# Four changes to the order of a fused linear-attention and maxout kernel: stores with slack, scores and y in pairs, wo's second half last, the last output in halves

## The chip, the cores and the metric

The kernel runs on one core of one Trainium2 chip. The metric is device time in microseconds (us) of one execution. Each kernel is executed several times; a run is called slow when it is more than 1.5% above the fastest of the same kernel, and only fast runs go into a ratio. Faster or slower asks for 2%.

A profile records one execution. Its span is shorter than the measured time by about 1.8 us, and it may fall on a run that is not typical.

## The reference, cut to what matters

```python
def _attn_ref(q, k, v, alpha):            # all (4, 8, 768, 48)
    state = zeros((B, H, D, D))
    for t in range(S):
        state = alpha[:, :, t, :, None] * state + einsum('bhd,bhe->bhde', k[:, :, t], v[:, :, t])
        y[:, :, t] = einsum('bhd,bhde->bhe', q[:, :, t], state)

def _moe_ref(x, w1, w2, w_out):           # x (3072, 384), w1 and w2 (384, 1024), w_out (1024, 384)
    return np.maximum(x @ w1, x @ w2) @ w_out

def reference(...):                       # x is y with heads side by side
    x = attn_out.transpose(0, 2, 1, 3).reshape(B * S, H * D)
    return _moe_ref(x, w1, w2, w_out)
```

The kernel cuts the tokens into 24 chunks of 128. In a chunk the recurrence becomes matmuls: cumulative sums of ln alpha (`cs`), transposes of scaled q and k (`tp`), the scores k·q (`pa`, `pb`), a masked copy of them (`pt`), and y from `pt` with v and from the carried state (`T`). The six chunks of the first batch go two at a time, as "double" chunks whose tiles begin with d (`dcs`, `dtp`, `dpa`, `dy`). The maxout uses max(h1, h2) = relu(x(w1 − w2)) + x w2. So it needs one product `h` of 384 × 1024 per token and a relu `g`; the second term is folded into a matrix `m` = w2·wo that is made once (`mp` in PSUM).

## The kernel before: what the change touches

The code in this section is shortened.

All instructions are put in order ahead of time by a small list scheduler. It keeps estimated times for the five engines; for each it picks, among the operations whose inputs and buffers will be ready, the one with the smallest (time, priority).

```python
def pick(self, e):
    now = self.free[e]
    best = None
    for op in self.todo[e]:
        t = self.start(op)
        if t is None:
            continue
        margin = self.MARGIN if e == "PE" and op.prio < 1000 else 0.0
        late = max(t + margin, now)
        key = (late, op.prio - (0.5 if op.tiled and self.tiled else 0.0))
        if best is None or key < best[0]:
            best = (key, max(t, now), op)
    return best
```

Operations marked `tiled` are the scores and y. Their matmuls use parts of TensorE's array (64 × 128 tiles for the scores, 128 × 32 for y); everything else uses the whole of it.

```python
def p3(n):                     # scores of a chunk, tiled=True
    for r in range(NP):
        for o, ps in ((0, pa), (64, pb)):
            nc.tensor.matmul(ps[:, r, :], lhsT=qk[o:o+D, NP+r, :], rhs=qk[o:o+D, r, :], start=True, stop=True)

def p4(n):                     # y of a chunk, tiled=True
    for b, x, is_t, start, stop in rounds(n % NCH == 0):
        ...                    # lhsT is 32 columns of T16 or of v16
        nc.tensor.matmul(y[o:o+32, b//4, :], lhsT=lhsT, rhs=rhs, start=start, stop=stop)
```

The output of 128 tokens takes eleven matmuls of 384 columns, a copy out of PSUM, and a store issued from SP, the queue that issues the loads too:

```python
def tstep(a, i, half):
    if half == 0:
        op = ops[t0] = psm.tile([128, DM], FP32, tag="m", name="op")
        for s in range(3):
            nc.tensor.matmul(op, lhsT=xT[:, s, t0:t0+C], rhs=m16[:, s, :], start=(s == 0), stop=False)
    op = ops[t0]
    for f in (range(3) if half == 0 else range(3, NF)):
        nc.tensor.matmul(op, lhsT=gts[a][:, f, i*C:(i+1)*C], rhs=wo16[:, f, :], start=False, stop=(f == NF-1))

def oevict(e, t0):
    outs[t0] = mo.tile([128, DM], FP32, tag="outs", name="outs", bufs=NO)     # NO = 4
    copy(e, outs[t0], ops[t0])

def store(t0):
    nc.sync.dma_start(out=out[t0:t0+C, :], in_=outs[t0])
```

The big loads have a fixed order, with each weight in two halves; `m` takes eight steps over the halves of w2 and wo:

```python
for x in "d0 w20 w21 wo0 w10 wo1 w11 d1 d2".split():
    ...
def prep_m(s, i):              # i: half of wo
    ...                        # mp: one PSUM tile for both halves
    for f in range(NFH*i, NFH*i + NFH):
        nc.tensor.matmul(mp, lhsT=w2T[:, f, s*128:(s+1)*128], rhs=wo16[:, f, :], start=(f == 0), stop=(f == NF-1))
```

The single chunks' loads of alpha, k, q and v reuse the space of the float32 weights. So in a profile "w2f<-in_alpha" is a load of alpha.

## Time and profile before

| kernel before | us |
|---|---|
| three executions | 148.53, 151.44, 147.98 |
| execution that was profiled | 151.01 |
| span of that profile | 149.2 |

The prediction below shows this profile's lines and reads them. Two things help to read it. The row "PE" of the 40 slices gives TensorE's busy share in tenths. A timeline line gives start, duration, engine, source line, operation, output and inputs, tile shape, operand shape, and how many alike were grouped. Matmuls overlap, so the distance between starts is what one costs, not its duration.

### The profile page before, as it was taken

What the parts mean: (1) busy time and instruction counts of PE and PEld (TensorE: products, weight loads), DVE (VectorE), ACT (ScalarE), POOL (GpSimd) and SP (SyncE); (2) the same over time, 40 slices, a digit from 0 to 9 for tenths busy, and PEclk for the clock granted to TensorE, in tenths of its full rate; (3) what the DMA queues carried; (4) which work ended last, traced back from release to release, by engine and by line L of the source; (5) the groups of instructions that cost most, each with busy time, mean ns of one, the idle gap of its engine ahead of it and who ended that gap; (6) DMA issues with size and microseconds to landing.
All of it is one profiled execution on the core that took longest, in us unless ns stands there. A gap on an engine that the chain in (4) does not pass through costs nothing.

```text
span 149.2 us, 4865 instructions
## 1 busy us (share of the span) xinstructions
PE 131.3 (88%) x1958; PEld 87.7 (59%) x1958; DVE 85.2 (57%) x161; ACT 100.8 (68%) x223; POOL 82.3 (55%) x184
## 2 busy tenths in 40 slices
PE   0275698799998968999999999999999999999990
PEld 0263555676776655766665666665665666656650
DVE  4745764577676676886476766679269693200000
ACT  4431876867784487778767996797768666935721
POOL 7975600769996269774088857657567963000000
PEclk9999999999999999999999999999999999999998
DMA  5989999999969699979899997989999861103112
GB/s 123 244 266 392 380 356 234 244 264 197 195 157 211 134 199 201 236 150 242 195 206 208 226 237 133 211 208 216 199 201 243 191 145 53 53 6 114 43 61 97
DMA packets 93543, 28.62 MB, mean 192 GB/s; under 512 B 87889, under 2 KB 91985, under 8 KB 93521
## 3 DMA queue, kind: packets, MB, share of 16 engines
q1 hardware_dynamic: 93520, 28.32, 80.0%
q8 instruction: 15, 0.25, 0.7%
q14 instruction: 8, 0.06, 0.1%
HBM read 23.59 MB, written 4.72 MB: 190 GB/s over the span
## 4 chain that ended last, share of the span: by engine, by line
PE 68%; SPq 14%; DMA 11%; ACT 2%; issue 1%; POOL 1%; DVE 0%; ACTq 0%; POOLq 0%; DVEq 0%
PE op L711 20%; PE h L694 19%; PE op L708 7%; SPq L203 7%; DMA dqf<-in_q_dram 6%; PE y L465 6%; PE pa L406 3%; DMA w1f<-in_alpha_dram 3%; SPq L223 3%; DMA w2f<-in_alpha_dram 3%; PE tp L388 3%; PE tp L390 2%; PE cs L330 2%; SPq L233 2%; PE kv L417 2%; SPq L194 2%
## 5 line engine op out<-in xcount | busy, mean ns | idle before, releaser
L711 PE MATMUL op<-wo,g 128*128 128x384 f16 x192 | 37.3, 326 | 0.0
L694 PE MATMUL h<-xT,wd 128*128 128x384 f16 (+1 forms) x216 | 36.6, 309 | 0.0
L701 ACT ACTIVATE g<-h 128x384 f16<-128x384 f32 (+1 forms) x53 | 23.8, 469 | 2.7 <-PE h L694 2.4
L694 PEld LDWEIGHTS <-wd 128*128 128x128 f16 x216 | 19.2, 98 | 9.2
L711 PEld LDWEIGHTS <-g 128*128 128x128 f16 x192 | 17.9, 98 | 11.3
L425 DVE TENSOR_TENSOR pt<-pa,u 128x512 f16<-128x512 f32 x18 | 12.4, 690 | 12.0 <-PE pb L406 6.5
L655 ACT COPY outs<-op 128x384 f32<-128x384 f32 x20 | 9.6, 480 | 13.8 <-PE op L711 13.8
L655 ACT COPY qk<-tp 128x1024 f16<-128x1024 f16 x15 | 15.2, 1016 | 1.7 <-PE tp L390 1.5
L367 POOL TENSOR_TENSOR T<-w,g 48x192 f16<-48x192 f32 x30 | 15.6, 520 | 1.2
L708 PE MATMUL op<-m,xT 128*128 128x384 f16 x72 | 15.6, 325 | 0.0
L425 DVE TENSOR_TENSOR pt<-pb,u 128x512 f16<-128x512 f32 x18 | 12.3, 683 | 0.1
L521 POOL TENSOR_TENSOR dkt<-dkf,den 128x384 f16<-128x384 f32 x6 | 6.3, 1058 | 9.8 <-ACT den L503 9.8
L469 ACT CAST xT<-y 128x384 f16<-128x384 f32 x18 | 8.7, 484 | 4.4 <-PE y L465 4.0
L352 POOL TENSOR_TENSOR kt<-wof,en 128x384 f16<-128x384 f32 x6 | 6.3, 1053 | 8.6 <-ACT en L340 6.3
L436 DVE TENSOR_TENSOR w<-kv,t 48x192 f32<-48x192 f32 x24 | 8.5, 353 | 3.9 <-PE kv L417 3.0
L699 DVE TENSOR_SCALAR g<-h 128x256 f16<-128x256 f32 (+1 forms) x19 | 8.6, 475 | 1.8 <-PE h L694 1.8
L340 ACT ACTIVATE en<-cs 128x384 f32<-128x384 f32 x18 | 9.0, 498 | 0.8 <-PE cs L334 0.8
L465 PE MATMUL y<-pt,v 128*32 128x128 f16 x288 | 9.0, 220 | 0.4 <-ACT outs L655 0.4
L340 ACT ACTIVATE ep<-cs 128x384 f32<-128x384 f32 x18 | 9.0, 502 | 0.0
L352 POOL TENSOR_TENSOR kt<-w1f,en 128x384 f16<-128x384 f32 x6 | 6.0, 1003 | 4.9 <-ACT en L340 2.4
L352 POOL TENSOR_TENSOR kt<-w2f,en 128x384 f16<-128x384 f32 x6 | 6.0, 1001 | 4.2 <-ACT en L340 3.3
L708 PEld LDWEIGHTS <-xT 128*128 128x128 f16 x72 | 6.4, 97 | 3.3
(121 smaller groups left out, 273.1 us busy)
## 6 DMA issues: line engine op xcount, KB each, us to landing
out_dram<-outs SPq DMA_DIRECT2D x24, 192.0 KB, 3.0
w2f<-in_moe_w_dram SPq DMA_DIRECT2D x2, 768.0 KB, 7.8
wof<-in_moe_w_out_dram SPq DMA_DIRECT2D x2, 768.0 KB, 11.2
w1f<-in_moe_w_dram SPq DMA_DIRECT2D x2, 768.0 KB, 12.2
dvf<-in_v_dram SPq DMA_DIRECT2D x3, 384.0 KB, 5.6
wof<-in_alpha_dram SPq DMA_DIRECT2D x6, 192.0 KB, 4.0
wof<-in_k_dram SPq DMA_DIRECT2D x6, 192.0 KB, 4.6
wof<-in_q_dram SPq DMA_DIRECT2D x6, 192.0 KB, 4.8
```

The costliest lines, as they stand in the source:

```text
L203: nc.sync.dma_start(out=dloads[m][i][:, hs], in_=src[0, hs, m * C2 : (m + 1) * C2, :].rearrange("h (p j) d -> p h (j d)", j=2),)
L340: nc.scalar.activation(out=t, in_=csv, func=ACTF.Exp, scale=scale)
L352: nc.gpsimd.tensor_mul(out=kts[n % NB][:, :, 0:D], in0=loads[n][1], in1=st[n]["en"])
L367: nc.gpsimd.tensor_mul(out=st[n]["T16"][ps, :, D * t : D * t + D], in0=st[n - 1]["w"][ps], in1=st[n]["g"][ps].unsqueeze(2).to_broadcast([D ...
L425: nc.vector.tensor_mul(out=s["pt"][:, t], in0=s["pp"][t], in1=ub)
L465: nc.tensor.matmul(y[o : o + 32, b // 4, :], lhsT=lhsT, rhs=rhs, start=start, stop=stop)
L469: nc.scalar.copy(out=xT[:, :, n * C : (n + 1) * C], in_=st[n]["y"])
L655: {"ACT": nc.scalar.copy, "DVE": nc.vector.tensor_copy, "POOL": nc.gpsimd.tensor_copy}[e](out=out, in_=in_)
L694: nc.tensor.matmul(h[:, 0:W], lhsT=wd16[:, s, f * 128 : (f + 1) * 128], rhs=xT[:, s, a : a + W], start=(s == 0), stop=(s == 2))
L701: nc.scalar.activation(out=gts[a][:, f, 0:W], in_=hs[a, f][:, 0:W], func=ACTF.Relu)
L708: nc.tensor.matmul(op, lhsT=xT[:, s, t0 : t0 + C], rhs=m16[:, s, :], start=(s == 0), stop=False)
L711: nc.tensor.matmul(op, lhsT=gts[a][:, f, i * C : (i + 1) * C], rhs=wo16[:, f, :], start=False, stop=(f == NF - 1))
```

## The change

Four intentions: (1) a store isn't issued until 3 us after it could be, so that loads overtake it, with six output buffers instead of four; (2) a ready scores or y group is held for up to 2.5 us until a second one is ready, so that both run in one stretch; (3) wo's second half is loaded after all of w1, and the first half of `m` isn't made until the first double chunk's y; (4) the last 128 tokens' output is made in two halves of 192 columns, so that the last copy and the last store are half as big.

```diff
-    def __init__(self, ..., tiled=False, after=()):
+    def __init__(self, ..., tiled=False, after=(), slack=0.0):
+    HOLD = 2.5
 ...
     def pick(self, e):
-        for op in self.todo[e]:
-            t = self.start(op)
+        ready = [(op, self.start(op)) for op in self.todo[e]]
+        hold = e == "PE" and not self.tiled and sum(op.tiled for op, t in ready if t is not None and t <= now + 0.1) < 2
+        for op, t in ready:
 ...
-            late = max(t + margin, now)
-            key = (late, op.prio - (0.5 if op.tiled and self.tiled else 0.0))
+            late = max(t + margin + op.slack, now)
+            prio = op.prio
+            if op.tiled and self.tiled:
+                prio -= 2.0
+            elif op.tiled and hold and now - t < self.HOLD and now > 45.0:
+                prio += 2000.0
+            key = (late, prio)
 ...
+    def tcols(a, i, c):        # half c of the last output: 3 + 8 matmuls of 192 columns
+    def ocols(e, t0, c):       # its copy
+    def scols(t0, c):          # its store: SP for the first half, ACT for the second
+        eng = nc.scalar if c else nc.sync
+        eng.dma_start(out=out[t0 : t0 + C, cs], in_=outs[t0][:, cs])
 ...
-    NG, NO = 3, 4
+    NG, NO = 3, 6
 ...
-    for x in "d0 w20 w21 wo0 w10 wo1 w11 d1 d2".split():
+    for x in "d0 w20 w21 wo0 w10 w11 wo1 d1 d2".split():
 ...
-                      ..., after=[prev],
+                      ..., after=[prev] if i else [],
+            if i == 0:
+                mfirst.append(prev)
 ...
+        if m == 0:
+            for o in mfirst:
+                o.after.append(g["p4", 0])
 ...
+            if a + i == NCG - 1:
+                for c in range(2):
+                    ... tcols, ocols (ACT), scols ...
+                continue
 ...
-            op("st", a + i, {"SP": 0.55}, ..., prio=-1)
+            op("st", a + i, {"SP": 0.55}, ..., prio=-1, slack=3.0 if a + i < NCG - 4 else 0.0)
```

More of the change, by code (lines that the diff above doesn't have):

```diff
@@ L16, with __init__ @@
 class Op:
-    def __init__(self, sched, name, n, engs, fn, deps=(), lat=0.1, alloc=(), reads=(), prio=0.0, tiled=False, after=()):
+    def __init__(self, sched, name, n, engs, fn, deps=(), lat=0.1, alloc=(), reads=(), prio=0.0, tiled=False, after=(), slack=0.0):
         self.name, self.n, self.engs, self.fn, self.lat = name, n, engs, fn, lat
@@ L22, in __init__ @@
         self.after = [d for d in after if d is not None]
-        self.done = None
+        self.done, self.slack = None, slack
         for b in list(alloc) + list(reads):
@@ L93, in pick @@
             margin = self.MARGIN if e == "PE" and op.prio < 1000 else 0.0
-            late = max(t + margin, now)
-            key = (late, op.prio - (0.5 if op.tiled and self.tiled else 0.0))
+            late = max(t + margin + op.slack, now)
[5 more added lines that the diff above has]
+            key = (late, prio)
             if best is None or key < best[0]:
-                best = (key, max(t, now), op)
+                best = (key, max(t + op.slack, now), op)
         return best
@@ L712, in tstep @@
                              start=False, stop=(f == NF - 1))
+    def tcols(a, i, c):
+        t0 = a + i * C
+        cs = slice(c * DM // 2, (c + 1) * DM // 2)
+        op = ops[t0, c] = psm.tile([128, DM], FP32, tag="m", name="opc")
+        for s in range(3):
+            nc.tensor.matmul(op[:, 0 : DM // 2], lhsT=xT[:, s, t0 : t0 + C], rhs=m16[:, s, cs], start=(s == 0), stop=False)
+        for f in range(NF):
+            nc.tensor.matmul(op[:, 0 : DM // 2], lhsT=gts[a][:, f, i * C : (i + 1) * C], rhs=wo16[:, f, cs],
+                             start=False, stop=(f == NF - 1))
+    def ocols(e, t0, c):
+        if c == 0:
+            outs[t0] = mo.tile([128, DM], FP32, tag="outs", name="outs", bufs=NO)
+        copy(e, outs[t0][:, c * DM // 2 : (c + 1) * DM // 2], ops[t0, c][:, 0 : DM // 2])
+    def scols(t0, c):
+        cs = slice(c * DM // 2, (c + 1) * DM // 2)
+        eng = nc.scalar if c else nc.sync
+        eng.dma_start(out=out[t0 : t0 + C, cs], in_=outs[t0][:, cs])
     outs = {}
@@ L795 @@
         w2t.append(op("w2te", f, {"DVE": 0.6, "ACT": 0.75}, lambda e, f=f: prep_te(e, f), deps=[t], reads=[b], prio=-0.4))
-    mdone = []
+    mdone, mfirst = [], []
     for s in range(3):
@@ L801 @@
             prev = op("m", s, {"PE": 0.66}, lambda e, s=s, i=i: prep_m(s, i), lat=0.17,
-                      deps=w2t[2 * i : 2 * i + 2] + woc[2 * i : 2 * i + 2], after=[prev],
+                      deps=w2t[2 * i : 2 * i + 2] + woc[2 * i : 2 * i + 2], after=[prev] if i else [],
                       alloc=[b] if i == 0 else (), reads=[b] if i else (), prio=0.4 + 0.01 * s)
+            if i == 0:
+                mfirst.append(prev)
         mdone.append(op("mev", s, {"ACT": 0.4, "DVE": 0.45}, lambda e, s=s: copy(e, m16[:, s, :], mps[s]),
@@ L970, in refill @@
             bo, bs = Buf(rm), Buf(ro)
+            if a + i == NCG - 1:
+                for c in range(2):
+                    b = (bo, Buf(rm))[c]
+                    o = op("t", a + i, {"PE": 0.95}, lambda e, a0=a0, i=i, c=c: tcols(a0, i, c), lat=0.17,
+                           deps=mdone + woc + rel, after=pend[-1:], alloc=[b], reads=[bg], prio=1000 + a)
+                    pend.append(o)
+                    ev = op("oev", a + i, {"ACT": 0.28}, lambda e, t=a0 + i * C, c=c: ocols(e, t, c), deps=[o],
+                            alloc=[] if c else [bs], reads=[b, bs] if c else [b], prio=n)
+                    op("st", a + i, {"ACT" if c else "SP": 0.3}, lambda e, t=a0 + i * C, c=c: scols(t, c), lat=1.2, deps=[ev],
+                       reads=[bs], prio=-1)
+                continue
             for half in range(2):
@@ L977, in refill @@
                     alloc=[bs], reads=[bo], prio=n)
-            op("st", a + i, {"SP": 0.55}, lambda e, t=a0 + i * C: store(t), lat=1.2, deps=[ev], reads=[bs], prio=-1)
+            op("st", a + i, {"SP": 0.55}, lambda e, t=a0 + i * C: store(t), lat=1.2, deps=[ev], reads=[bs], prio=-1, slack=3.0 if a + i < NCG - 4 else 0.0)
         return True
```

## The prediction

> **What bounds the kernel now.** I read the page's engine shares and 40 slices first, then the busy time by windows, then TensorE's waits, then its timeline at the changes between kinds of matmul, and last the chain of waits and the DMA landings.
>
> The page: the PE row is full from about slice 17 to the last, DMA is full until slice 32.
>
> ```profile
> PE 131.3 (88%) x1958; PEld 87.7 (59%) x1958; DVE 85.2 (57%) x161; ACT 100.8 (68%) x223; POOL 82.3 (55%) x184
> PE   0275698799998968999999999999999999999990
> DMA  5989999999969699979899997989999861103112
> ```
>
> Windows of 5 us (first figure after the length is PE's busy time): idle sits before 30 us and in 45 to 60, and from 60 to 145 there is none.
>
> ```profile
> 25.00:30.00 5.00, 3.85 (x46) 3.10 (x44) 2.79 (x5) 4.33 (x12) 2.94 (x3) 1.00 1.04 249
> 45.00:50.00 5.00, 4.33 (x125) 3.14 (x124) 3.06 (x7) 3.34 (x8) 3.05 (x7) 1.00 0.94 201
> 50.00:55.00 5.00, 3.77 (x58) 2.78 (x56) 3.67 (x8) 2.43 (x8) 2.22 (x6) 1.00 0.74 147
> 55.00:60.00 5.00, 4.39 (x69) 3.00 (x67) 3.42 (x7) 3.80 (x12) 4.23 (x8) 1.00 0.98 212
> 60.00:65.00 5.00, 5.00 (x81) 3.24 (x78) 3.89 (x8) 4.09 (x8) 3.43 (x8) 1.00 0.95 204
> ```
>
> PE's waits in 45 to 60 us are for ln of alpha, for the cast of v and once for a free PSUM bank; behind the first two stand loads (the groups name the DMA of alpha into w2f's and w1f's space and of v). A busy figure that counts overlapping tails hides part of it: by start times PE lost about 0.83 us at 46.4, 1.0 at 52, 0.5 at 53.2 and 0.77 at 57.2, together 3.1 us.
>
> ```profile
> PE cs L330 <- ACT loga L325: 1.3, 2, 0.7
> PE kv L417 <- POOL v L356: 0.9, 1, 0.9
> PE y L465 <- ACT outs L655: 0.4, 1, 0.4
> ```
>
> So the end is the sum of PE's work after 60 us, of what PE loses before 60, and of the tail. But "busy" from 60 on is not all matmul. The timeline shows what a change of tiling costs:
>
> ```profile
> 61.03 0.98 PE L711 MATMUL op<-wo,g 128*128 128x384 f16 x5
> 61.94 0.23 PE L406 MATMUL pa<-qk 48*128 48x128 f16 x1
> ...
> 62.12 0.22 PE L406 MATMUL pb<-qk 48*128 48x128 f16 x1
> 62.27 0.40 PE L388 MATMUL tp<-ident,qt 128*128 128x128 f16 x4
> ...
> 65.35 0.28 PE L465 MATMUL y<-pt,v 128*32 128x128 f16 x5
> 65.56 0.23 PE L406 MATMUL pa<-qk 48*128 48x128 f16 x1
> ```
>
> Output matmuls start every 0.163 us, so five end at 61.84; the scores start at 61.94: 0.10 lost. From the last score (62.12) to the transpose (62.27) is 0.15 where transposes follow each other at 0.056: 0.095 lost. From the last y (65.35 plus 0.28 less its own 0.22, so 65.41) to the scores (65.56) 0.15 again: y (128x32 tiles) and scores (64x128 tiles) differ too. Each change of tile shape costs some 0.095 us, whatever the two shapes.
>
> The tail, from the chain and the landings: last matmul group 144.46 to 145.77, the copy 145.84 to 146.32, the store issued at 146.34, landed at 148.20, span 149.2.
>
> ```profile
> 144.46 1.31 PE op L711 x8
> 145.77 0.03 ACTq L655
> 145.80 0.04 issue
> 145.84 0.48 ACT outs L655
> ```
>
> **What the Trainium skill says.** "TensorEngine Tiling (Array Packing)", section Key Properties: "Changing tiling mode (not just tile) drains the TensorE". The trace agrees and gives the size, 0.095 us. "TensorE: Matmul & The Clock Gate", part 1: the array's clock halves after about 3.4 us idle and returns after as long a busy stretch. Here transposes step at 0.107 us before 21.8 us and at 0.056 later, and no idle of up to 1.1 us brought the slow step back; that matters below. "DMA: Bandwidth & Descriptors", section Issuing engines are not separate DMA queues: DMAs from SP and ACT share the same 16 engines, and a second issuer saves only issue time; before issues from SP alone, so no run here shows it.
>
> **The change part by part.**
>
> *Scores and y together.* A ready tiled group is held up to 2.5 us (after the scheduler's own 45 us) until two are ready; once in tiled mode the bonus is 2 instead of 0.5. I counted changes of tile shape in the two programs' instruction orders: 87 before, 76 after. Before, 7 of the 18 single chunks' score groups stood next to a y; after, all 18 do (14 y then scores, 4 scores then y). 11 x 0.095 = 1.05 us off PE, nearly all after 60 us where PE has no other slack: it comes off the end. Matmul counts are otherwise the same (72 h of 256 and 144 of 384 columns in both).
>
> *Stores with slack.* A store may not be issued until 3 us after it could, except the last four, so loads go first; outs grows from 4 to 6 buffers for it. Where it matters is 41.9 to 43.9: two stores (41.88 and 43.18) stand before chunk 8's alpha (issued 42.66, landed 46.58) and k. After, alpha, k and q of chunk 8 precede the first store. A 192 KB transfer takes 0.65 to 0.95 us of the queue here, so alpha lands one transfer earlier or a little more, about 45.2 to 45.9, and the 0.83 us wait at 46.4 goes. The bytes don't change and DMA is full until 120 us, so by the ninth chunk's alpha (the 36th DMA in both orders, landed 52.67) nothing is gained. The new PE order now asks for exactly that load before anything else: after the common prefix (which ends at 51.7) it has the cumulative sum of chunk 9, where before had scores, kv and y. PE gets there at about 51.3 and can go on at 52.67 + 0.1 + 0.53 (ln) = 53.3: 2.0 us idle, in place of before's 1.0 + 0.5 at nearly the same place, with 0.5 us of work (scores, kv) not yet done. At the next such point (chunk 10's alpha, 57.24 in before) the new order has more to do first and waits about 0.25 in place of 0.77. Together 45 to 60: 3.1 becomes about 2.25, gain 0.85.
>
> *wo's second half last.* w1's second half now lands about 21.1, wo's about 23.9 (before the reverse: 21.07 wo, 23.93 w1). The second 12 matmuls of w2.wo need it: casts end about 24.8 instead of 21.9. The first 12 now run together, to about 23.1 (four at 0.32, eight at 0.163 from 20.48); then PE idles 1.7 us, too short for the clock, and the other 12 x 0.163 end at 26.75. Before, the stream ended at 25.2 and chunk 2's cumulative sums waited for alpha until 25.78. They slip by 0.95; den, dep and POOL's dkt with them. But PE then waited 0.92 for dqt until 28.54, which was held by q's landing (27.83). Now dep ends at 28.3 in place of 27.3, so dqt starts 0.4 later, and PE's transposes start about 28.95: 0.45 lost net. It pays into the wait at 46.4 which the earlier alpha has removed, so I count it whole: +0.45.
>
> *Last tokens by halves.* 11 matmuls of 384 columns become 22 of 192, 0.081 each if the step scales (256 columns step at 0.109): no cost. Copies of 256 columns take 0.39 and of 384 0.49 us in the relu groups, so 192 take about 0.34: 0.15 off the last copy. The last store is half the bytes: full stores took 1.86 us from issue to landing, of which perhaps 0.2 goes. 0.35 us together, all of it on the end. It is issued from ACT, which has nothing else left.
>
> Sum: -1.05 - 0.85 + 0.45 - 0.35 = -1.8 us. Of 148.5 that makes 146.7. I take 146.6, since the schedule was surely picked to be better than this reading of its first part.
>
> **Rivals.** (1) *The hold creates new waits.* PE runs strictly in order; pulling scores next to y ties a chunk's y to its masks on DVE, and the relus on ACT are now clumped. For it: three PSUM banks feed h, op and y. Against: DVE is at 57%, ACT at 68%, the scheduler still asks for 0.25 us of margin per group, and its previous order has no wait at all from 60 on. If each of the 18 pairs waited 0.1, 1.8 us would be back: 148.5, same. (2) *DMA becomes the bound.* It runs at 0.9 to 1.0 until 120 us; if PE is faster the loads don't come faster. Against: PE has 22 us of pure feed-forward after 124 us, so a backlog is there to fill holes; only the start, where there is none, can starve. If the first part loses what the switches gain: 148. (3) *The load phase gains more.* If chunk 9's alpha also lands an us earlier (41 to 43 DMA was at 0.45), the 2.0 us of idle halve: 145.5. (4) *The reordered weights are worse than I think*, the clock falling back in the 1.7 us gap: h and dcs at half speed for 3.4 us would add about 1.5: 148.
>
> **Range and chances.** Switches and tail, 1.4 us, are sure to 0.3. The first 60 us are sure to about 1.2 either way[...]. The runs of before spread from 147.98 to 151.44. So 145.2 to 148.3 for 8 in 10. 2% is 3 us; the sum would need the optimistic first part too: 0.2. Slower by 2% needs both rival 1 and 4: 0.03. Same: 0.77.
>
> **What would show it.** The timeline: y and scores adjacent, 0.15 between them, 3 changes for each pair. Windows 60 to 145 still 5.00 each; if some are at 4.5, rival 1. PE's waits: the one for w2f's alpha at 46 gone, a wait of 1 to 2 us at chunk 9's cumulative sum near 51 to 53 (if absent, rival 3), a gap of 1.7 near 23 to 24.8 before the second half of mp, transposes of chunk 2 at 28.95. The tail: last copy about 0.34, end of the last matmul to the span's end 3.0 in place of 3.4. I am wrong if PE's stretch from 60 to its end is not 1 us shorter in sum of gaps.

## The result, and the profile after

The changed kernel took 146.69 us (median of four runs, 146.62 to 146.77), and the kernel before, beside it, 148.58 (147.98 to 151.44). The ratio of the fast runs is 0.9886 (95% interval 0.9856 to 0.9916). A ratio here is the mean time of one kernel's fast runs over the mean time of the other's fast runs of the same rounds, so it is not quite the ratio of the medians. The predicted time, 146.6 us, was met within 0.1 us. What follows shows that not all of its terms were.

The page of the changed kernel, its summary line of the engines and two rows of the 40 slices:

```profile
PE 129.7 (90%) x1969; PEld 89.4 (62%) x1969; DVE 86.6 (60%) x163; ACT 99.1 (68%) x222; POOL 83.0 (57%) x184
PE   0376884899999999999999999999999999999991
DMA  4999999999989898999997999999899852010213
```

PE has eleven matmuls more (22 narrow ones in place of 11) and is full from slice 9 on. The dent of before in slices 13 to 16 ("8968") is gone.

The same stretch by windows of 5 us, changed kernel (length, then busy time of PE, PEld, DVE, ACT, POOL with their counts, PE's clock, DMA share, GB/s):

```profile
45.00:50.00 5.00, 5.00 (x132) 3.65 (x130) 2.74 (x7) 3.30 (x8) 3.70 (x9) 1.00 0.93 219
50.00:55.00 5.00, 4.82 (x103) 3.88 (x101) 3.99 (x8) 5.00 (x13) 3.76 (x8) 1.00 1.00 194
```

PE is busy for 9.82 us of these ten, where the profile of before had 8.10. That looks like the gain from the earlier loads which the prediction expected. The first experiment shows that it isn't.

The timeline of PE at a pair, changed kernel:

```profile
57.42 0.22 PE L414 MATMUL pb<-qk 48*128 48x128 f16 x1
...
57.53 0.22 PE L414 MATMUL pb<-qk 48*128 48x128 f16 x1
57.68 0.24 PE L473 MATMUL y<-qk,T 112*32 112x128 f16 x4
...
57.99 0.28 PE L473 MATMUL y<-pt,v 128*32 128x128 f16 x5
58.20 0.99 PE L719 MATMUL op<-wo,g 128*128 128x384 f16 x5
```

Scores and y now stand together: 0.15 us from the last score to the first y (57.53 to 57.68) where scores follow each other every 0.055, so the change of shape between two tiled forms costs 0.095, as predicted. A pair has three changes where two separate groups have four.

PE's waits in 15 to 30 us, and the only one listed in 40 to 142 us, changed kernel (engine, tile and line, what it waited for, total us, times, longest):

```profile
PE mp L691 <- ACT wo L663: 2.3, 1, 2.3
PE dtp L541 <- DVE dqt L527: 0.7, 1, 0.7
...
PE tp L396 <- ACT qk L663: 0.2, 1, 0.2
```

The first is the predicted gap for wo's second half, longer than the 1.7 us foreseen since the first twelve matmuls of `m` ended at 21.29 instead of about 23.1. The predicted 2.0 us wait for chunk 9's alpha near 51 to 53 us isn't there: that load landed at 49.84, its logarithm was done at 50.45, and PE asked for it at 50.51.

The end, from the chain that ended last (start, duration, what), changed kernel:

```profile
141.01 0.25 PE opc L728 x3
141.25 0.67 PE opc L730 x8
141.93 0.02 issue
141.95 0.32 ACT outs L663
```

The last copy took 0.32 us where before's took 0.48, and the last store 1.66 us from its issue on ACT (142.30) to landing (143.96) where before's took 1.86.

### The profile page after: what moved, and what is told of

It reads as the page before. It is cut to its first block, busy times and chain, and to the rows that moved or that the text cites. A ratio compares the mean times of both kernels' runs of the same rounds, so it can differ in the third digit from the quotient of the medians.

```text
span 144.9 us, 4890 instructions
## 1 busy us (share of the span) xinstructions
PE 129.7 (90%) x1969; PEld 89.4 (62%) x1969; DVE 86.6 (60%) x163; ACT 99.1 (68%) x222; POOL 83.0 (57%) x184
## 3 DMA queue, kind: packets, MB, share of 16 engines
q1 hardware_dynamic: 93520, 28.22, 82.0%
## 4 chain that ended last, share of the span: by engine, by line
PE 73%; DMA 12%; SPq 6%; ACT 5%; issue 1%; DVE 1%; ACTq 0%
PE h L702 21%; PE op L719 19%; DMA wof<-in_moe_w_out_dram 9%; PE op L716 7%; PE y L473 6%; PE pa L414 4%; DMA w2f<-in_alpha_dram 3%; PE tp L396 3%; SPq L231 3%; PE tp L398 2%; SPq L211 2%; PE cs L338 2%; PE kv L425 1%; PE mp L691 1%; PE dtp L541 1%; PE opc L730 1%
## 5 line engine op out<-in xcount | busy, mean ns | idle before, releaser
L719 PE MATMUL op<-wo,g 128*128 128x384 f16 x184 | 35.4, 326 | 0.0
L719 PEld LDWEIGHTS <-g 128*128 128x128 f16 x184 | 17.2, 98 | 11.5
L663 ACT COPY qk<-tp 128x1024 f16<-128x1024 f16 x14 | 14.4, 1025 | 1.7 <-PE tp L398 1.7
L716 PE MATMUL op<-m,xT 128*128 128x384 f16 x69 | 15.0, 326 | 0.0
```

The source lines that it names most:

```text
L663: {"ACT": nc.scalar.copy, "DVE": nc.vector.tensor_copy, "POOL": nc.gpsimd.tensor_copy}[e](out=out, in_=in_)
L716: nc.tensor.matmul(op, lhsT=xT[:, s, t0 : t0 + C], rhs=m16[:, s, :], start=(s == 0), stop=False)
L719: nc.tensor.matmul(op, lhsT=gts[a][:, f, i * C : (i + 1) * C], rhs=wo16[:, f, :], start=False, stop=(f == NF - 1))
```

## The experiments

Twelve runs were made in three batches of four, each batch with eleven runs of the kernel before beside it; the medians of these were 147.71, 147.81 and 148.47 us. The record names chip 6 for the first batch (e0_before, u_pair, u_wo, u_tail) and chip 5 for the other two. All gave the right result.

| run | what it is | median us | ratio to before (95%) |
|---|---|---|---|
| e0_before | before, again | 148.11 | 1.0045 (1.0003 to 1.0088) |
| u_pair | after, without the pairing | 147.69 | 1.0020 (0.9972 to 1.0069) |
| u_wo | after, old order of the weights' loads | 146.52 | 0.9938 (0.9905 to 0.9971) |
| u_tail | after, last output whole | 147.15 | 0.9981 (0.9933 to 1.0029) |
| e1_after | after, again | 147.01 | 0.9927 (0.9885 to 0.9969) |
| u_slack | after, without the stores' slack | 147.03 | 0.9935 (0.9887 to 0.9983) |
| late_before | before, with an extra load first | 149.26 | 1.0116 (1.0066 to 1.0165) |
| late_after | after, with the same load | 148.42 | 1.0031 (0.9978 to 1.0084) |
| sw_untiled | after, 36 more changes of shape | 151.15 | 1.0180 (1.0129 to 1.0231) |
| sw_same | the same matmuls without changes | 147.97 | 0.9986 (0.9935 to 1.0037) |
| pair_tail | before with pairing and halves only | 147.19 | 0.9911 (0.9864 to 0.9959) |
| pair_only | before with pairing only | 147.68 | 0.9969 (0.9911 to 1.0026) |

The first row is the yardstick: the same kernel against itself gave 1.0045, with an interval that leaves out 1 although nothing differs. So the intervals are narrower than the real scatter, and differences of half a per cent between rows say little. The profiles had to carry the argument. I cut each span at two places: the start of the second double chunk's first transposes (`dtp`, where PE goes on after the weights are prepared), and PE's last end. I also added up, from about 46 us on, what each change of tile shape costs beyond the normal step, and (last column) PE's waits: what is left of the longer steps between starts of matmuls.

| profile | start of that dtp | from it to PE's end | PE's end to the span's end | cost of all changes of shape | waits after 46 us |
|---|---|---|---|---|---|
| before (slow run) | 28.54 | 117.22 | 3.47 | | 2.97 |
| e0_before | 28.26 | 114.28 | 3.48 | 6.22 | 0.00 |
| after | 28.23 | 113.69 | 3.01 | 5.08 | 0.65 |
| u_pair | 28.11 | 114.83 | 3.01 | 6.32 | 0.44 |
| u_wo | 28.28 | 113.43 | 3.01 | 5.08 | 0.41 |
| u_tail | 27.78 | 113.41 | 3.47 | 5.08 | 0.41 |
| e1_after | 28.03 | 114.08 | 3.02 | | 1.04 |
| u_slack | 28.57 | 113.30 | 3.02 | 5.22 | 0.11 |
| late_before | 29.72 | 114.27 | 3.40 | | 0.00 |
| late_after | 29.39 | 113.45 | 2.96 | | 0.42 |
| sw_untiled | 28.18 | 118.55 | 3.01 | | 0.42 |
| sw_same | 27.93 | 115.28 | 3.01 | | 1.82 |
| pair_tail | 27.73 | 114.66 | 3.01 | | 1.47 |
| pair_only | 27.66 | 115.99 | 3.48 | | 1.68 |

### e0_before: was the profile of before typical?

No edit: the kernel before, once more, with five rounds.

> The kernel before once more, for a profile of the fast state (the one at hand fell in a run of 151.0 us). Theory A: the slow run lost its time in the early DMAs; a fast profile has a span of about 146.8 us (148.6 less the 1.8 that lies between span and time in the changed kernel), w2's first half lands at about 11.4 us instead of 12.8, and PE's waits in 45 to 60 us shrink from 3.1 to 2 us or less. Theory B: those waits belong to the order of stores and loads; they stay near 3 us in the fast profile too, and the 2.5 us that the slow run lost lie before 20 us or are spread.

Measured: the profile was of a fast run this time, 147.78 us with a span of 146.0. Its windows, same columns as above:

```profile
45.00:50.00 5.00, 5.00 (x132) 3.61 (x130) 2.75 (x7) 3.62 (x8) 3.70 (x9) 1.00 0.94 188
50.00:55.00 5.00, 5.00 (x80) 3.84 (x78) 4.43 (x11) 4.29 (x12) 3.33 (x7) 1.00 0.95 202
```

PE is busy without a break in both, and no wait of PE is listed between 40 and 142 us. The 3.1 us of idle time that the prediction found in 45 to 60 us, and from which it promised 0.85 us back, belonged to the slow run. There chunk 8's alpha landed at 46.58 and chunk 9's at 52.67 us; here they landed at 43.50 and 47.45. The column "from it to PE's end" says the same: 117.22 in the slow run, 114.28 here, a difference of 2.94. So the honest comparison is e0_before with after, fast with fast: spans of 146.0 and 144.9. Of their difference of 1.08 us (by unrounded times), 0.46 is the tail and 0.6 is PE's stretch.

### u_pair: take the pairing away

```diff
             if op.tiled and self.tiled:
-                prio -= 2.0
-            elif op.tiled and hold and now - t < self.HOLD and now > 45.0:
+                prio -= 0.5
+            elif False and now - t < self.HOLD and now > 45.0:
                 prio += 2000.0
```

> The changed kernel without the pairing of scores and y (88 changes of tile shape instead of 76). Theory A (each change costs 0.095 us of a PE that has no slack): 12 x 0.095 = 1.15 us longer than the changed kernel, 147.8. Theory B (the hold makes waits that eat what it saves): no longer than 146.7. Theory C (the pairing is the whole gain): 148.5.

Measured: ratio 1.0020. The changes of shape cost 6.32 us (88 changes), 1.24 more than with pairs. PE's stretch is 114.83. The remaining three parts of the change together gained nothing that these runs can show, although the shortened tail (3.01) is in this kernel.

### u_wo and u_tail: undo one small part each

u_wo:

```diff
-    for x in "d0 w20 w21 wo0 w10 w11 wo1 d1 d2".split():
+    for x in "d0 w20 w21 wo0 w10 wo1 w11 d1 d2".split():
```

> The changed kernel with wo's second half loaded before w1's again. Theory A (my prediction): loading it last costs 0.45 us at the end, so this takes 146.25. Theory B: the 0.8 us that PE gains before 30 us are given back in the wait for chunk 9's alpha near 50 us, which the changed kernel meets with almost no wait; then 146.6 to 146.7. Theory C (the change's intent): loading it last gains; then 147.0 or more.

u_tail:

```diff
-            if a + i == NCG - 1:
+            if False:
```

> The changed kernel with the last tokens' output whole again. Theory A: the tail from PE's last matmul to the span's end goes from 3.0 back to 3.45 us and the time from 146.7 to 147.1 or 147.15. Theory B: the halves cost on PE (22 matmuls instead of 11) what they save behind it; then 146.7.

Measured for u_wo: the transposes start at 28.28, against 28.23 with wo last and 28.26 in e0_before. The predicted 0.45 us isn't there. Over all fast profiles that start scatters more than this: 27.78 to 28.57 with wo last, 27.66 to 28.28 with the old order, the two delayed runs left out. Its median, 146.52, is the lowest of all rows, but its ratio (0.9938) and that of e1_after (0.9927, on another chip) have nearly the same interval, so no version is shown to be better.

Why the delay vanished: PE's waits before 30 us in e0_before,

```profile
PE dtp L533 <- DVE dqt L519: 1.6, 1, 1.6
...
PE mp L683 <- ACT wo L655: 0.5, 1, 0.5
```

sit in the other place: 1.6 us at `dtp` and 0.5 at `mp` here, 0.7 and 2.3 in the changed kernel. (The sum is 0.9 larger there since PE came to this stretch 0.8 us earlier: the scores of the first double chunk start at 15.02 in place of 15.82.) By the timeline the cumulative sums `dcs` are at 25.52 in place of 24.60, so the 0.92 us of delay is real up to there; at `dtp` it is gone. `dqt` needs two things, `dep` from ACT and the load of q. Here is `dep`, POOL's `dkt` and `dqt` in the timeline of e0_before,

```profile
25.60 0.48 ACT L503 ACTIVATE dep<-dcs 128x384 f32<-128x384 f32 x1
25.83 1.95 POOL L521 TENSOR_TENSOR dkt<-dkf,den 128x384 f16<-128x384 f32 x2 [9.20 <-ACT den L503]
...
27.04 1.16 DVE L519 TENSOR_TENSOR dqt<-dqf,dep 128x384 f16<-128x384 f32 x1 [2.59 <-ACT dgg L511]
```

and of the changed kernel:

```profile
26.52 0.48 ACT L511 ACTIVATE dep<-dcs 128x384 f32<-128x384 f32 x1
26.75 2.28 POOL L529 TENSOR_TENSOR dkt<-dkf,den 128x384 f16<-128x384 f32 x2 [10.91 <-ACT den L511]
...
27.04 1.13 DVE L527 TENSOR_TENSOR dqt<-dqf,dep 128x384 f16<-128x384 f32 x1 [1.41 <-ACT dep L511]
```

In e0_before `dep` was done at 26.08, but q landed at 26.94, and `dqt` started 0.09 us later. (Its line names `dgg`, which it doesn't use. But in all six profiles with the old order of loads, and in two with wo last, `dqt` starts 0.093 or 0.094 us after q's landing.) In the slow run the chain names q itself:

```profile
19.24 8.59 DMA dqf<-in_q_dram
27.92 0.57 DVE dqt L519
```

In the changed kernel `dep` was done at 27.00, 0.92 later, and q had landed at 26.79. So `dqt` started at 27.04 in both: it had stood idle for q before, and the delay used up that room of 0.86 us. That the two starts agree to 0.01 us is chance, since q landed 0.15 earlier.

`dqt` then takes 1.16 and 1.13 us, where it took 0.56 in the slow run. A `dkt` takes 1.00 us by itself, and one is under way each time: in e0_before the second, which ends at 27.78, in the changed kernel the first, which ends at 27.75. `dqt` ends 0.41 to 0.42 us after that, here and in u_wo (27.81 and 28.22). The Trainium skill, "SBUF — State Buffer", section "SBUF: two separate sides", says that a DVE operation with two SBUF inputs and a GpSimd operation that reads SBUF exclude each other for a whole instruction, and the later one "fully blocks". These ends agree. The lock lengthens `dqt` in both kernels by nearly the same, so it isn't what absorbed the delay.

Measured for u_tail: ratio 0.9981; PE's end to the span's end is 3.47 against 3.01. Its chain's end,

```profile
139.89 1.31 PE op L719 x8
141.20 0.03 ACTq L663
141.23 0.04 issue
141.27 0.48 ACT outs L663
```

has the 0.48 us copy of before. The halves are worth 0.46 us at the end of the span, against 0.35 predicted; the copy gives 0.16, the store 0.20, and the rest lies in smaller gaps between them. The span of u_tail is 144.7 all the same, as its transposes started 0.45 us early: one profile can't resolve half a microsecond by its span, but the cut can.

### e1_after and u_slack: are the stores' slack and the gain real?

e1_after has no edit.

> The changed kernel once more, beside the kernel before on the same chip, for a ratio from more runs. From the two fast profiles: tail 0.46 us shorter, PE's stretch from 28.25 us to its end 0.6 us shorter, so 1.05 of 147.7: ratio 0.993. If the first measurement (0.9886) holds, 1.1% shorter; then something beside those two is gained in most runs of before that its fast profile does not show.

u_slack:

```diff
-            op("st", ..., prio=-1, slack=3.0 if a + i < NCG - 4 else 0.0)
+            op("st", ..., prio=-1, slack=0.0)
```

> The changed kernel without the slack of the stores (77 changes of tile shape instead of 76). My prediction: chunk 8's alpha one transfer later, PE's wait near 46 us comes back, up to 0.85 us longer than the changed kernel. Theory from the fast profile of before, which has no wait of PE in 45 to 60 us with its stores ahead: no difference beyond the one change (0.1 us).

Measured: 0.9927 with the slack and 0.9935 without it, on the same chip. PE's stretch is even a little shorter without (113.30 against 113.69 and, in e1_after, 114.08). No gain from the slack is shown; that it helps in slow runs like the one first profiled stays possible, as no slow run of u_slack was profiled.

### late_before and late_after: do late loads bring the waits back?

My first theory of the slow run was that its loads came late, which the PE order didn't tolerate. The test adds one load of 512 KB ahead of the weights to both kernels:

```diff
+    late = constp.tile([128, 2, FH], FP32)
+
     def load_w2(i):
+        if i == 0:
+            nc.sync.dma_start(out=late, in_=moe_w1.rearrange("(s p) f -> p s f", p=128)[:, 0:2, 0:FH])
         load_w(moe_w2, w2f, slice(i * FH, (i + 1) * FH))
```

> The kernel before with one extra load of 512 KB (into a tile that nothing reads) ahead of the weights: every later load lands some 1.3 us later, as in the slow run that I predicted from; the order of instructions is the same. Theory (the waits of 45 to 60 us come from late loads): they are there again, 2 to 3 us together, and the time is about 150 to 151. Rival (the slow run was slow for another reason): PE moves by the 1.3 us once, before 30 us, and no wait stands in 45 to 60: 149.

> The changed kernel with the same extra load. My prediction's reading of late loads: wait at 46 gone, a wait of about 2 us at chunk 9's cumulative sum, 0.45 lost before 30 us; 0.4 us better than the kernel before in the first 60 us, so in all about 1.8 us below the run of before with the late loads. Rival: the new order takes late loads much better (waits under 1 us in 45 to 60): 3 us or more below it. Other rival: no better: 1.1 us below, as in the fast state.

Measured: 1.0116 and 1.0031. The theory fell in this form. The late load moves everything before 30 us by about 1.4 us (the transposes start at 29.72 in place of 28.26), PE simply starts later too, and its stretch after that is unchanged: 114.27 against 114.28. The waits of 45 to 60 us don't come back. In the slow run the landings weren't late by a constant: against e0_before they fell from 1.2 us behind near 35 us to 5.2 behind at 52.7. What slowed the transfers of that run stays open. What is settled is that the kernel's order alone doesn't produce those waits. The gain of after over before is the same under the delay: 1.0031/1.0116 = 0.9916.

### sw_untiled and sw_same: what does one change of shape cost?

sw_untiled puts one 128 × 128 matmul of two columns into the middle of every single chunk's scores; its result is overwritten by the scores that follow. That makes 36 more changes. sw_same puts in the same matmul in the scores' own tile shape.

```diff
         for r in range(NP):
+            if r == 2:
+                nc.tensor.matmul(pa[:, 3, 0:2], lhsT=ident16, rhs=ident16[:, 0:2], start=True, stop=True)      # sw_untiled
+                nc.tensor.matmul(pa[:, 3, 0:2], lhsT=ident16[0:64, :], rhs=ident16[0:64, 0:2], start=True, stop=True)   # sw_same
             for o, ps in ((0, pa), (64, pb)):
```

> The changed kernel with one two-column matmul on the whole array in the middle of each of the 18 score groups (into columns of PSUM that the group writes afterwards; results stay right, order unchanged): 36 more changes of tile shape. Theory A (a change costs 0.095 us and PE has no slack): 18 x (2 x 0.095 + 0.025) = 3.9 us more, stretch from the first transposes of chunk 2 to PE's last matmul 117.3 to 117.9, time about 150.8. Theory B (the drains would partly hide in waits that are there anyway): under 2 us more.

> The control: the same extra matmul, but in the tile shape of the scores, so no change of shape. Theory A: 18 x 0.03 = 0.5 us more at most, stretch about 114, time about 147.3. If it costs as much as the one on the whole array, it is the extra matmul and not the change of shape that costs.

Measured, PE's timeline of sw_untiled at one of them:

```profile
58.99 0.22 PE L416 MATMUL pb<-qk 48*128 48x128 f16 x1
59.14 0.18 PE L414 MATMUL pa<-ident 128*128 128x2 f16 x1
59.25 0.23 PE L416 MATMUL pa<-qk 48*128 48x128 f16 x1
```

and of sw_same:

```profile
58.36 0.22 PE L416 MATMUL pb<-qk 48*128 48x128 f16 x1
58.41 0.17 PE L414 MATMUL pa<-ident 64*128 64x2 f16 x1
58.41 0.22 PE L416 MATMUL pb<-qk 48*128 48x128 f16 x1
```

In the first the untiled matmul starts 0.15 us after the score before it, and the next score 0.11 later; in the second it starts after 0.05. Over the 18 groups the scores of sw_untiled took 3.88 us longer than without, 0.216 a group, and those of sw_same 0.47, 0.026 a group. So two changes cost 0.216 − 0.026 = 0.190, and one 0.095 us. PE's whole stretch agrees: 118.55 − 115.28 = 3.27 us for 36 changes, 0.091 each. The times agree as well: 151.15 − 147.97 = 3.2. Both agree only because the two profiles lost nearly the same to waits, 1.69 us (1.21 of it at 41.1 us for ln of alpha) and 1.82; these waits also made both stretches longer than expected. The count inside the groups doesn't depend on them.

### pair_tail and pair_only: the parts forward from before

pair_tail is before plus the pairing and the halves (edits: the old load order, the delay of `m` taken out, slack 0; the six output buffers stay). pair_only is that with the last output whole.

```diff
-    for x in "d0 w20 w21 wo0 w10 w11 wo1 d1 d2".split():
+    for x in "d0 w20 w21 wo0 w10 wo1 w11 d1 d2".split():
-                      ..., after=[prev] if i else [],
+                      ..., after=[prev],
-        if m == 0:
-            for o in mfirst:
-                o.after.append(g["p4", 0])
-            op("st", ..., slack=3.0 if a + i < NCG - 4 else 0.0)
+            op("st", ..., slack=0.0)
-            if a + i == NCG - 1:          # pair_only alone
+            if False:
```

> Only two of the four parts: pairing (77 changes of tile shape) and the last tokens by halves; stores without slack and wo's second half loaded as in the kernel before. If slack and load order win nothing, it is as fast as the changed kernel or 0.3 us faster (the run without slack had no wait for a relu on ACT at 67 and 110 us): stretch 113.3, tail 3.0, time 146.2 to 146.9. If they carry part of the gain: 147.3 or more.

> Pairing alone, the last tokens' output whole. By the traces: stretch 113.3 instead of before's 114.27, tail 3.47, so 1.0 us below the kernel before, about 146.8. If the tail's halves carry the gain: no faster than before.

Measured: 0.9911 with both, 0.9969 with the pairing alone. By their times the two parts reproduce the gain of the whole change (0.9886 and 0.9927) without slack and without the new load order. The profiles don't show it: pair_tail's PE stretch is 114.66, where 113.3 was expected and before had 114.28, because 1.47 us of waits stand in it. pair_only's interval includes 1, so the pairing alone is not shown to gain time. Its profile fell on its slowest run (148.90 us, span 147.1), with a wait of 1.0 us for ln of alpha at 41.8 us that only sw_untiled has too. Its PE stretch, 115.99, is therefore no measure of the pairing.

## Why the prediction was right, and where it wasn't

**The changes of shape: right.** Predicted 11 × 0.095 = 1.05 us; the cost of all of them fell from 6.22 to 5.08, by 1.14, and the direct test gives 0.095 for one. Not all of it reached the end: PE's stretch fell by 0.59 (114.28 to 113.69) in this pair of profiles, by 0.85 in u_wo and by 0.98 in u_slack.

**Rival 1 was there.** The difference is new waits of PE that the list of waits mostly hides, as matmul ends overlap. By start times the changed kernel loses 0.345 us at 53.0 before the transposes, for a copy on ACT, and 0.15 each at 67.1 and 110.4 inside long rows of `h`. The timeline there shows fifteen `h` matmuls in a row and the relus on ACT one after the other behind them, each of which must empty a PSUM buffer:

```profile
65.77 2.75 PE L702 MATMUL h<-xT,wd 128*128 128x384 f16 x15
...
66.82 1.28 ACT L709 ACTIVATE g<-h 128x384 f16<-128x384 f32 x3
```

That makes 0.645, and 1.14 − 0.645 = 0.5 against the 0.59 measured. The same sum is 1.14 − 0.41 = 0.73 for u_wo, 1.0 − 0.11 = 0.89 for u_slack and −0.10 − 0.44 = −0.54 for u_pair (which loses 0.44 to ln of alpha), where the stretches changed by 0.85, 0.98 and −0.55. The 1.8 us that rival 1 put at stake did occur, though in a few waits and not as 0.1 at each pair: sw_same, which has the changed kernel's order, lost 1.82 us after 46 us, pair_tail 1.47 and e1_after 1.04, where the kernel before lost nothing in its two fast profiles, with and without the extra load. In e1_after only 0.2 of the stretch's gain remained. The largest single wait, 0.62 to 0.69 us near 55 to 57 us, stands in four profiles with pairs, and is for a copy of `xT` on ACT. In pair_tail:

```profile
PE h L702 <- ACT xT L477: 0.5, 1, 0.5
PE cs L338 <- ACT loga L333: 0.3, 1, 0.3
PE tp L396 <- ACT qk L663: 0.2, 1, 0.2
```

So the saving on changes of shape is in every profile, and from a tenth of it to more than all of it is given back. That the pairing makes these waits is likely but not shown: u_pair lost 0.44 without pairs, and no run held the landings of the loads fixed.

**The prediction's own sign of being wrong came up.** It asked for PE's stretch from 60 us on to be 1 us shorter in sum of gaps. By start times the changes of shape and waits after 60 us come to 5.24 us in the profile that it was made from, 4.84 in e0_before and 4.32 in the changed kernel: 0.92 shorter, or 0.52 fast with fast.

**The tail: right mechanism, size off.** 0.46 us in place of 0.35: the smaller store saved the 0.2 that was allowed for it, the copy 0.16, and the gaps around them a little more. The Trainium skill, "DMA: Bandwidth & Descriptors", section Issuing engines are not separate DMA queues, says that a second issuer saves only issue time. That agrees: the last half store issued from ACT landed after 1.66 us, the half store from SP after 1.62.

**The stores and the load phase, −0.85: the step that failed.** "3.1 becomes about 2.25" took the waits of one slow run for a property of the kernel. In a fast run they were zero before the change and so could not be gained; e0_before shows it, and u_slack shows no loss without the slack. The sub-step of a new 2.0 us wait at chunk 9's alpha failed with it, since it took the slow run's landing of 52.67, where fast runs had 47.45 (e0_before) and 49.84 (after). The order of issues did change as predicted, with chunk 8's alpha, k and q ahead of the first store, but this alpha landed at 43.98, not earlier than e0_before's 43.50. Nor did the missing wait near 51 to 53 us mean rival 3, as the prediction had it: the time didn't fall to 145.5.

**wo's second half last, +0.45: failed too.** The gap in `mp` came, at 2.3 us. But the transposes behind it start at 28.23 in place of the predicted 28.95. The slip of 0.95 us up to `dep` was right (0.92 measured). The step "dqt starts 0.4 later" failed, for the same reason as the one above: it took q's landing from the slow run, 27.83, which left `dqt` about half a microsecond of room. In the fast run q landed at 26.94 with `dep` done at 26.08, and the room was 0.86. Rival 4 (a falling clock) didn't occur: the transposes at 28 us and later step at the same 0.056.

**Two readings were off.** The 3.1 us of idle time hold two changes of shape; without them the waits are 0.83 + 0.92 + 0.45 + 0.77 = 2.97. And PE's work after 124 us isn't pure feed-forward: groups of y stand at 124.74 and 131.49 in the profile that the prediction read.

**So hitting the number within 0.1 us was partly luck.** The two failed terms, −0.85 and +0.45, left −0.40, and the base of 148.5 was at the upper end of what the three later batches gave for the same kernel (147.71, 147.81, 148.47). Without the failed terms the working says −1.4; the profiles of fast runs say −1.08; the ratio of e1_after says −0.7% (1.08 us of 147.8) and that of the first result −1.1% (1.7 us). These two intervals overlap. How much of the difference between them is chance can't be told from runs whose own yardstick is off by 0.45%.

**What stays open:** whether the slack or the load order helps in the slow state; whether the pairing makes the waits near 50 to 57 us; what slowed the loads of the first profile; and whether u_wo, with the lowest median, is in truth the best version. No kernel here beats the changed one by more than the scatter.

## What to carry to other kernels

Before a wait in a profile is counted as something to gain, look at the state of the run that was profiled and at a second profile: here 3 us of waits stood in the one slow execution that was profiled, and in no fast one of the same kernel. A cost that is paid many times and can be counted in the instruction order (changes of tile shape, 0.095 us each) is the firmer ground; multiply it out, then look at starts of instructions, not at busy time, for what is given back. A delay ahead of a join (an instruction with two inputs) counts only by what exceeds the wait for the other input, and that wait must come from a run in the right state: here 0.92 us vanished in the wait for q.

## What the Trainium skill lacked or had wrong

- "TensorEngine Tiling (Array Packing)", section Key Properties, says that a change of tiling mode drains TensorE but gives no size. Here one change cost 0.095 us in the direct test and 0.089 to 0.097 in the kernels' own places, between two tiled shapes (64 × 128 and 128 × 32) as well as between tiled and whole.
- "SBUF — State Buffer", section "SBUF: two separate sides", has the lock between DVE and GpSimd right: the DVE multiplication ended 0.41 to 0.42 us after the end of the GpSimd one in three profiles. I found no page that says how the lock looks in a profile: not as idle time of DVE but as a longer instruction (0.56 to 1.28 us for the same `dqt` here).
- I found no page that says by how much loads vary between executions of the same kernel. Here the same alpha landed at 47.45 us in a fast run and 52.67 in a slow one, and an identical kernel measured 1.0045 against itself.
